# A retention and feed-forward kernel: a new load and cast prologue, a block-diagonal state product, score matmuls placed beside value matmuls, and the queries of the first four chunks loaded on the ScalarE queue

## The chip, the cores and the metric

The kernel runs on one core of one Trainium2 chip. The metric is device time in microseconds (us). The kernel before takes 239.28 us, the median of three runs (238.09 to 240.16). Each run is marked fast or slow; unless a text says otherwise, the runs compared here are fast ones.

"The profile" is a recording of one run of a kernel on the chip. PE is the matmul engine (TensorE), PEld its weight loads, DVE is VectorE, ACT is ScalarE, POOL is GpSimd, SP is SyncE. A name with a q behind it, such as ACTq, is the sequencer of that engine, which also issues DMA transfers. "Span" is the time from the first to the last instruction of the core; a timed run is longer than its span here (237.42 against 235.7 for the profiled run of before).

## The reference

```python
# q, k, v: 4 batches, 8 heads, 768 positions, 64 channels; fp32
gamma = 1.0 - 2.0 ** (-5.0 - np.arange(H))
for t in range(S):
    state = gamma * state + outer(k[:, :, t], v[:, :, t])     # 64 x 64 per head
    y[:, :, t] = (1 / sqrt(D)) * (q[:, :, t] @ state)
x = y.transpose(0, 2, 1, 3).reshape(B * S, H * D)              # 3072 x 512
h = np.maximum(x @ w_in, 0)                                    # w_in: 512 x 2048
return (h * h) @ w_out                                         # w_out: 2048 x 512
```

## The kernel before

The 3072 rows are cut into 24 chunks of 128, six for each batch. For a chunk, k is scaled by a decay factor and cast (`a_cast`), k and q are transposed on PE (`a_turn`), the masked scores inside the chunk are made (`a_score`), and `a_out` adds the state product (what earlier chunks of the batch contribute), the value product, and the update of the state. The feed-forward (`f1`, `f2`) takes four chunks at a time, in groups of four matmuls of 512 columns; the attention pieces of the next four chunks are woven between these groups. The parts that the argument touches:

```python
    blocks = [[0, 1], [2, 3]]          # then four chunks each
    # ... cut
    def load_chunk(m):
        b, i = divmod(m, NCH)
        got = []
        for name, src, dt in (("kn", k, FP32), ("qs", q, BF16), ("vs", v, BF16)):
            t = ldpool.tile([P, H, D], dt, tag=name, name=f"{name}{m}")
            eng = nc.sync if dt == FP32 else nc.gpsimd       # GpSimd's loads cast on the way
            eng.dma_start(t[:], src[b, :, i * C : (i + 1) * C, :].rearrange("h s d -> s h d"))
            # ... cut
    # ... cut: load_chunk(0) to (3) and constants between them, then the four slices of w_in,
    #     all on GpSimd's queue but k
    # in a_out(m): the state product, eight matmuls of 64x64
        if i > 0:
            s_bf = state["s"]
            for p in range(NP):
                for hh in range(2):
                    r = slice(64 * hh, 64 * hh + 64)
                    nc.tensor.matmul(yt[r, p, :], lhsT=s_bf[r, p, :], rhs=kqT[r, 1, p, :],
                                     start=(p == 0), stop=False, skip_group_check=True)
    # ... cut
    def stages(ms):                    # the order of the pieces that are woven in
        seq = []
        for n in range(len(ms) + 2):
            if 0 <= n - 1 < len(ms):
                seq.append(lambda m=ms[n - 1]: a_score(m))
            if n < len(ms):
                seq.append(lambda m=ms[n]: a_cast(m))
                seq.append(lambda m=ms[n]: a_turn(m))
            if 0 <= n - 2 < len(ms):
                seq.append(lambda m=ms[n - 2]: a_out(m))
        return seq
```

## Time and profile before

| profiled run of before | value |
|---|---|
| time, span | 237.42 us, 235.7 us (this run is 1.9 us under the median) |
| PE's first work | 9.55 us |
| first feed-forward matmul | 22.68 us |
| four blocks of four chunks | 35.09, 34.87, 34.75, 35.10 us |
| last block, nothing woven in | 27.79 us |
| end of PE, then the last store | 232.06 us, 3.6 us |

Two rows of the page of before. A digit is the busy share of one fortieth of the span, in tenths; PEclk is the granted clock of TensorE.

```profile
PE   0166997799999999999999999999999999999993
...
PEclk9999999999999999999999999999999999999999
```

PE is full from about slice 9 to the end (a slice is 5.9 us). The losses lie in the first fifth.

The chain of waits of before, two pieces of its first 25 us (start, length, what); the pieces ahead of them are mostly GpSimd issuing the loads of q and v. The chain runs back from the last instruction through whatever released each step.

```profile
11.97 10.67 DMA w_in_bf_93<-in_moe_w_in_dram
22.68 1.03 PE hp_0_348 L282 x4
```

The feed-forward can't start before the first slice of w_in is there, and that slice takes 10.67 us from its issue. Its first packet moves at 16.3, 4.3 us after the issue: until then GpSimd's queue carries the q and v loads that stand ahead of w_in. After that it shares the DMA engines with the loads of the chunks. The DMA view of before for 17 to 22 us shows how (queue, packets, MB, share of the engines); q0 is GpSimd's queue, with w_in, and q1 is Sync's, with k:

```profile
q0 software_dynamic: 913, 0.76, 93.3%
q1 hardware_dynamic: 839, 0.21, 32.0%
```

Both queues move about the same number of packets, but those of q1 have 256 bytes (0.21 MB over 839), so Sync's queue gets about 42 GB/s (0.21 MB in 5 us).

The table of windows of before: the stretch, its length, the busy time (and instructions) of PE, PEld, DVE, ACT and POOL, then granted clock, DMA share and GB/s.

```profile
22.68:45.37 22.69, 19.83 (x217) 15.63 (x218) 13.26 (x38) 14.81 (x36) 11.06 (x13) 1.00 1.59 190
...
99.55:134.42 34.87, 34.82 (x281) 16.84 (x280) 16.24 (x28) 17.05 (x28) 7.01 (x8) 1.00 0.70 91
...
204.27:232.06 27.79, 27.79 (x129) 12.44 (x127) 6.81 (x16) 11.95 (x20) 0.00 (x0) 1.00 0.10 38
```

A block of four chunks (34.87 us) is the 27.79 us of its feed-forward and 7.1 us of attention for the next four chunks, and PE is busy in all of it, by ends that are modelled. So in these blocks only less PE work helps, or less of the loss between its pieces, which this column doesn't show (next).

One chunk's `a_out` in such a block, from the timeline of PE in before (start, length, line, output and inputs, shapes). A matmul's recorded end is modelled, so read the distances between starts.

```profile
130.06 1.03 PE L301 MATMUL op_1700<-w_out_bf_97,h_3_1355 128*128 128x512 bf16 x4
131.01 0.41 PE L225 MATMUL yt_1705<-kqT_1596,s_1691 64*64 64x128 bf16 x8
131.35 0.41 PE L236 MATMUL yt_1705<-pt_1655,vs_1345 128*64 128x128 bf16 x8
131.60 0.29 PE L252 MATMUL c_1530<-vs_1345,ks_1573 128*64 128x64 bf16 x8
131.82 1.04 PE L301 MATMUL op_1700<-w_out_bf_98,h_3_1355 128*128 128x512 bf16 x4
```

The feed-forward group takes 0.95 us to the next start where two such groups in a row take 0.86: about 0.1 us is lost on entering this piece, which has another shape. The state product takes 0.34, the value product 0.25, the state update 0.22.

Entering the transposes, whose shape is the feed-forward's 128x128, costs nothing in itself (0.86, for example from 120.44 to 121.30). But in each full block those of the second and third chunk start 1.05 us after the group ahead of them, because the cast of k is not done (timeline of before; the group ahead starts at 105.61):

```profile
106.66 0.23 PEld L184 LDWEIGHTS <-ks_1413 128*128 128x128 bf16 x4 [0.51 <-DVE ks_1413 L171]
106.66 0.40 PE L184 MATMUL tp_1429<-ident,ks_1413 128*128 128x128 bf16 x4
```

That is 0.19 us, six times in the three blocks: 1.1 us.

### The profile page before, as it was taken

The page shows a single profiled execution, that of the slowest core. Times are in us where ns is not written, and L with a number is a line of the kernel's source. Part 1 is how long each engine was busy: PE and PEld are TensorE (multiplying, and loading weights), DVE is VectorE, ACT ScalarE, POOL GpSimd, SP SyncE. Part 2 cuts the span into 40 slices and gives each one's busy share as a digit, 9 for nine tenths or more (in the row PEclk, how much of TensorE's full clock was granted, in tenths as well). Part 3 has the DMA queues.
Part 4 walks back from the last instruction along what each step waited for, and adds up shares of the span by engine and source line. Part 5 has one row for each costly group of instructions (what it writes and reads, how often), then busy time and mean ns, then how long its engine had stood idle before and what let it go on. Part 6 is the DMA issues. An engine that isn't in the chain of part 4 may idle for free.

```text
span 235.7 us, 4145 instructions
## 1 busy us (share of the span) xinstructions
PE 214.2 (91%) x1728; PEld 110.9 (47%) x1728; DVE 101.4 (43%) x188; ACT 109.6 (46%) x190; POOL 51.5 (22%) x82
## 2 busy tenths in 40 slices
PE   0166997799999999999999999999999999999993
PEld 0145785454544444444445544444544554444441
DVE  0446665642356533356634266534266524144100
ACT  2292586432277721277722277621377622277221
POOL 8983155642410102410203410100000000000000
PEclk9999999999999999999999999999999999999999
DMA  8999999998994087993078992041170011100112
GB/s 130 215 191 197 198 181 190 185 161 127 138 183 79 3 89 87 111 185 65 4 88 91 112 194 54 2 64 47 46 178 4 0 47 46 63 29 0 42 47 89
DMA packets 82579, 23.34 MB, mean 99 GB/s; under 512 B 75392, under 2 KB 79488, under 8 KB 82560
## 3 DMA queue, kind: packets, MB, share of 16 engines
q0 software_dynamic: 54144, 10.49, 52.7%
q1 hardware_dynamic: 28416, 12.59, 20.3%
q8 instruction: 13, 0.21, 0.4%
q14 instruction: 6, 0.05, 0.1%
HBM read 27.26 MB, written 6.29 MB: 142 GB/s over the span
## 4 chain that ended last, share of the span: by engine, by line
PE 85%; DMA 5%; POOL 4%; DVE 2%; ACT 1%; issue 1%; ACTq 0%; POOLq 0%
DMA w_in_bf_93<-in_moe_w_in_dram 5%; PE op_2057 L301 2%; PE op_1641 L301 2%; PE op_1232 L301 2%; PE op_865 L301 2%; PE op_795 L301 2%; PE op_2470 L301 2%; PE op_2411 L301 2%; PE op_762 L301 2%; PE op_2378 L301 2%; PE op_1549 L301 2%; PE op_1140 L301 2%; PE op_2529 L301 2%; PE op_2008 L301 2%; PE op_1975 L301 2%; PE op_1700 L301 2%
## 5 line engine op out<-in xcount | busy, mean ns | idle before, releaser
L282 PEld LDWEIGHTS <-w_in_bf_93 128*128 128x128 bf16 x112 | 10.6, 101 | 9.6 <-DMA w_in_bf_93<-in_moe_w_in_dram 1.0
L282 PEld LDWEIGHTS <-w_in_bf_95 128*128 128x128 bf16 x112 | 10.5, 98 | 9.3
L282 PEld LDWEIGHTS <-w_in_bf_94 128*128 128x128 bf16 x112 | 10.6, 98 | 8.9
L282 PEld LDWEIGHTS <-w_in_bf_96 128*128 128x128 bf16 x112 | 10.3, 98 | 8.2
L290 DVE TENSOR_TENSOR h_6_2567<-h_6_2567 128x512 bf16<-128x512 bf16 x16 | 6.8, 426 | 10.1 <-ACT h_6_2567 L289 10.1
L290 DVE TENSOR_TENSOR h_5_2177<-h_5_2177 128x512 bf16<-128x512 bf16 x16 | 6.8, 424 | 9.4 <-ACT h_5_2177 L289 9.4
L290 DVE TENSOR_TENSOR h_4_1774<-h_4_1774 128x512 bf16<-128x512 bf16 x16 | 6.8, 424 | 9.4 <-ACT h_4_1774 L289 9.4
L290 DVE TENSOR_TENSOR h_2_939<-h_2_939 128x512 bf16<-128x512 bf16 x16 | 6.8, 423 | 9.4 <-ACT h_2_939 L289 9.4
L290 DVE TENSOR_TENSOR h_3_1355<-h_3_1355 128x512 bf16<-128x512 bf16 x16 | 6.8, 424 | 8.9 <-ACT h_3_1355 L289 8.9
L301 PEld LDWEIGHTS <-h_6_2567 128*128 128x128 bf16 x64 | 6.3, 98 | 7.5
L184 PE MATMUL tp_172<-ident,ks_170 128*128 128x128 bf16 x4 | 0.6, 307 | 9.6 <-DVE ks_170 L171 9.6
L301 PEld LDWEIGHTS <-h_4_1774 128*128 128x128 bf16 x64 | 5.8, 98 | 6.5
L301 PEld LDWEIGHTS <-h_2_939 128*128 128x128 bf16 x64 | 5.8, 98 | 6.5
L301 PEld LDWEIGHTS <-h_5_2177 128*128 128x128 bf16 x64 | 5.8, 98 | 6.5
L301 PEld LDWEIGHTS <-h_3_1355 128*128 128x128 bf16 x64 | 5.8, 98 | 6.5
L290 DVE TENSOR_TENSOR h_1_528<-h_1_528 128x256 bf16<-128x256 bf16 x16 | 4.6, 291 | 4.8 <-ACT h_1_528 L289 3.7
L290 DVE TENSOR_TENSOR h_0_347<-h_0_347 128x256 bf16<-128x256 bf16 x16 | 4.5, 291 | 4.8 <-ACT h_0_347 L289 3.5
L184 PEld LDWEIGHTS <-ks_170 128*128 128x128 bf16 x4 | 0.3, 130 | 9.5 <-DVE ks_170 L171 9.5
L301 PEld LDWEIGHTS <-h_1_528 128*128 128x128 bf16 x32 | 2.8, 98 | 3.1
L158 ACT ACTIVATE yf<-t_f,lnp 128x128 f32<-128x128 f32 (+1 forms) x8 | 4.2, 603 | 0.0
L301 PEld LDWEIGHTS <-h_0_347 128*128 128x128 bf16 x32 | 2.9, 98 | 2.8
L83 POOL DMA_DIRECT2D vs_2173<-in_v_dram x1 | 0.9, 876 | 13.9 <-PE c_1530 L252 13.9
(803 smaller groups left out, 516.5 us busy)
## 6 DMA issues: line engine op xcount, KB each, us to landing
w_in_bf_93<-in_moe_w_in_dram POOLq DMA_DIRECT2D x1, 512.0 KB, 10.7
w_in_bf_94<-in_moe_w_in_dram POOLq DMA_DIRECT2D x1, 512.0 KB, 13.2
w_in_bf_95<-in_moe_w_in_dram POOLq DMA_DIRECT2D x1, 512.0 KB, 15.2
w_in_bf_96<-in_moe_w_in_dram POOLq DMA_DIRECT2D x1, 512.0 KB, 17.1
w_out_bf_97<-in_moe_w_out_dram POOLq DMA_DIRECT2D x1, 512.0 KB, 17.6
w_out_bf_98<-in_moe_w_out_dram POOLq DMA_DIRECT2D x1, 512.0 KB, 13.7
w_out_bf_99<-in_moe_w_out_dram POOLq DMA_DIRECT2D x1, 512.0 KB, 11.8
w_out_bf_100<-in_moe_w_out_dram POOLq DMA_DIRECT2D x1, 512.0 KB, 11.6
```

What stands on the lines that cost most here:

```text
L83: eng.dma_start(t[:], src[b, :, i * C : (i + 1) * C, :].rearrange("h s d -> s h d"))
L158: nc.scalar.activation(yf[:, p, lo:hi], t_f[:, lo:hi], AF.Exp, scale=lnp[:, p : p + 1])
L184: nc.tensor.transpose(tp[:, j, p, :], src[:, 2 * p : 2 * p + 2, :], ident[:])
L282: nc.tensor.matmul(hp[:, :n], lhsT=w_in_bf[s][:, cb, r * P : (r + 1) * P], rhs=xts[b][:, cb, :n], start=(cb == 0), stop=(cb == NCB - 1),)
L290: nc.vector.tensor_mul(h2[:, fb, :n], h2[:, fb, :n], h2[:, fb, :n])
L301: nc.tensor.matmul(op[:], lhsT=h2s[b][:, fb, j * P : (j + 1) * P], rhs=w_out_bf[part][:, r, :], start=(fb == 0), stop=(fb == NFB - 1),)
```

## The change

The intent is to shorten the front and to take PE work out of the blocks.

- q, k and v of the first eight chunks come as fp32 on hardware queues, and engines cast them (q of chunks 0 to 3 on ScalarE, v on GpSimd). GpSimd's queue is then free for w_in. The queries of chunks 0 to 3 go over ScalarE's queue: q0 and q1 at the start, q2 and q3 after the second transposes, behind the copy of `kqT1` in ScalarE's stream. k and v of chunks 0 to 3 go over Sync's.
- Filler matmuls on a zero tile are meant to keep PE's clock up (`Z`). The order of the first 8 chunks is written out by hand (`run`), with blocks of 2, 2, 1, 3 and then 4 chunks.
- The state is kept block-diagonal for each pair of heads: four matmuls of 128x128 instead of eight of 64x64, at the price of a second small copy on ScalarE.
- From chunk 12 on, the score of chunk m+1 stands directly behind the value product of chunk m, and the cast runs one round ahead of its transposes.

Smaller edits come with it: some constants are filled on VectorE instead of GpSimd, and buffer counts differ.

```diff
-    blocks = [[0, 1], [2, 3]]
+    for n in (2, 2, 1, 3, 4, 4, 4, 4):
 ...
-    load_chunk(0)
+    load(nc.sync, "k", 0)
+    load(nc.scalar, "q", 0)
+    load(nc.sync, "v", 0)
+    load(nc.scalar, "q", 1)
+    for m in range(1, 4):
+        load(nc.sync, "k", m)
+        load(nc.sync, "v", m)
 ...  (in a_cast)
+        if m < FIRST:                                    # FIRST = 8
+            if m < 4:
+                nc.scalar.activation(qs[m][:], qn.pop(m)[:], AF.Copy)
+            else:
+                nc.gpsimd.tensor_copy(qs[m][:], qn.pop(m)[:])
+            nc.gpsimd.tensor_copy(vs[m][:], vn.pop(m)[:])
 ...  (in a_out)
-                for hh in range(2):
-                    r = slice(64 * hh, 64 * hh + 64)
-                    nc.tensor.matmul(yt[r, p, :], lhsT=s_bf[r, p, :], rhs=kqT[r, 1, p, :], ...)
+                nc.tensor.matmul(yt[:, p, :], lhsT=s_bd[i % 2][:, p, :], rhs=kqT[:, 1, p, :], ...)
 ...
+        if after is not None:
+            a_score(after)
 ...  (the prologue: K cast, T turn, S score, P out, Y decay fill, Z filler, F f1, G f2)
+    run("Y0 Z12 K0 T0 Y1 Z2 K1 S0 Z2 T1")
+    load(nc.scalar, "q", 2)
+    load(nc.scalar, "q", 3)
+    run(" P0 K2 S1 Y2 Z2 T2")
+    load_w_in(0)
+    load_w_in(1)
+    run("P1 K3 S2 Y3 Z2 T3 P2 S3 Y4 Z4")
+    for s in (2, 3):
+        load_w_in(s)
 ...  (w_out, then k, q, v of chunks 4 to 7, held until slice 2 of w_out has landed)
+    run("F0.0 P3 Y5 F0.1 F0.2 F0.3 F1.0 F1.1 F1.2 F1.3")
 ...
+    run("K4 G0.3 G1.3 G2.3 K5 T4 G3.0 S4 G3.1 T5 G3.2 P4 S5 G3.3 K6")
 ...
-            if n < len(ms):
-                seq.append(lambda m=ms[n]: a_cast(m))
-                seq.append(lambda m=ms[n]: a_turn(m))
+            if m + 1 < NCHUNK:
+                seq.append(lambda m=m: a_turn(m + 1))
+            if m + 2 < NCHUNK:
+                seq.append(lambda m=m: cast(m + 2))
+            seq.append(lambda m=m: a_out(m, m + 1 if m + 1 < NCHUNK else None))
```

## The prediction

> **What bounds it now.** From about 47 us to 232 us TensorE is the limit: the table of windows shows PE busy 10.0 of each 10 us, and a steady block of four chunks takes 34.9 us (64.5 to 204.2 us, four blocks). Of that, 32 feed-forward groups of four 512-column matmuls at 0.864 us are 27.7 us; attention takes 7.2, 1.8 us a chunk. The loss is in front. In the timeline TensorE does nothing until 9.55 us and starts the feed-forward at 22.68 us, when the first w_in slice lands (10.7 us after issue, in the chain of waits). From there to the end of TensorE (232.1) are 209.4 us, of which I count 204 as work; the rest is a cold start (the first 256-column matmuls take 213 ns each, from 25.8 us on 110) and waits for chunk casts near 38 to 43 us (PE busy 3.4 of 5 us, 8.6 of 10).
>
> **What changes in the steady part.** (a) The state product: 8 matmuls of 64x64 (0.35 us) become 4 of 128x128; four such transposes take 0.22 us: -0.13 us a chunk. (b) Score directly behind value saves one entry gap of about 0.1 us from chunk 12 on. (c) The cast is now one round ahead of its transposes; before, about half of them waited 0.1 to 0.2 us. Together about -0.25 us a chunk over 20 chunks: -5 us. ScalarE gains one small copy a chunk (0.37 us now); at 48% busy that costs nothing.
>
> **What changes in front.** q, k, v of chunks 0 to 3 come as fp32 on hardware queues, which move 230 to 240 GB/s when alone (packet records, 2 to 4 us): 256 KB in 1.1 us, so v2 lands near 11.3 us. Casts go to ScalarE (q, est. 0.6 us, from the 128x512 output copy) and GpSimd (v, est. 0.8 us, unmeasured). w_in then starts about where it does now, 12 us, but with nothing ahead of it in its queue: landing near 18 instead of 22.7. The new limit is the attention chain through ScalarE: per chunk 1.0 us eviction, 0.6 cast, 1.3 decay fill; and the issue of q2 and q3 stands behind the second eviction, near 11.5 us. That is late: once w_in packets flow, the trace shows hardware-queue packets alternating 1:1 with w_in's (154 against 154 per us, 39 GB/s, 17 to 26 us); the Trainium skill's "DMA: Bandwidth & Descriptors", Queues, rings and completion order, describes this round robin. q3 may thus take 6.5 us instead of 1.1, landing near 20.5; then cast, fill, eviction, score, filler: feed-forward starts near 25 (22.4 if q3 is early, 28 if q2 suffers too). By then only the last value product of the four chunks is left.
>
> **Sum.** Start 25 + work left about 199 + stalls 3 (cold clock, decay fill holding relus, the one-chunk block) + tail 3.6 = 230.6 us of span, against 235.7; with the same 2 to 3 us outside the span: 233. The fillers should warm the clock (skill, "TensorE: Matmul & The Clock Gate", Part 1: a few us of activity), if idle gaps do not undo it.
>
> **Checks.** Steady block near 33.8 us; state product near 0.22 us; q3 landing 6 us or more after issue; first feed-forward matmul 22 to 28 us; no wait for k4.
>
> **What would make it wrong.** q2 and q3 landing before w_in flows (then 230); both crawling, with a cold TensorE (237); slow GpSimd casts delaying w_in.
>
> Chances: faster by over 2% 0.66, within 2% 0.29, slower 0.05. Predicted 233, range 228 to 237.5.

## The result, and the profile after

The changed kernel takes 230.12 us, the median of four runs (229.41 to 230.88), against 239.03 us for the kernel before in the same rounds (four runs). The ratio is 0.9626, with a 95% interval of 0.9571 to 0.9681. Ratios here are the mean time of one kernel's fast runs over that of the other's fast runs of the same rounds, so not quite the quotient of the medians. The profiled run (229.41 us) is the fastest of the four.

The page of after:

```profile
span 227.6 us, 4271 instructions
...
PE   7649799999879999999999999999999999999993
...
PEclk9997999999999999999999999999999999999999
```

PE works from the first slice on (fillers), and its clock falls in the fourth slice.

The chain of waits of after, long pieces in the first 25 us:

```profile
10.22 3.35 DMA qn_246<-in_q_dram
...
23.42 1.28 ACT yf_169 L175 x4
```

w_in has left the chain. In its place stand the load of q2 (`qn_246`), issued at 10.22, and ScalarE's work.

The timeline of after at these places (sequencer, engines; in brackets the idle time before and what ended it):

```profile
10.22 0.37 ACTq L91 DMA_DIRECT2D qn_246<-in_q_dram  x1
10.63 0.60 ACTq L91 DMA_DIRECT2D qn_248<-in_q_dram  x1
11.35 0.89 POOL L96 DMA_DIRECT2D w_in_bf_96<-in_moe_w_in_dram  x1
13.59 0.63 ACT L207 ACTIVATE qs_274<-qn_246 128x512 bf16<-128x512 f32 x1 [1.47 <-DMA qn_246<-in_q_dram]
14.27 0.40 PE L220 MATMUL tp_297<-ident,qs_274 128*128 128x128 bf16 x4 [1.82 <-ACT qs_274 L207]
21.25 0.60 PE L319 MATMUL hp_0_443<-xt_250,w_in_bf_96 128*128 128x256 bf16 x4
25.16 0.60 PE L319 MATMUL hp_0_499<-xt_250,w_in_bf_96 128*128 128x256 bf16 x4 [1.20 <-ACT h_0_442 L326]
```

ScalarE waits 1.47 us for q2, and PE 1.82 us for the cast of q2. The feed-forward starts at 21.25. At 25.16 PE waits 1.20 us, because the decay fill at 23.42 (in the chain above) holds ScalarE, which has to take the feed-forward's results out of PSUM.

How the queues shared the DMA engines in after: first 10.5 to 14 us, where q10 is ScalarE's queue with q2 and q3, q1 Sync's, and q0 w_in's:

```profile
q10 hardware_dynamic: 2064, 0.52, 65.7%
q1 hardware_dynamic: 1323, 0.33, 41.9%
q0 software_dynamic: 22, 0.02, 4.6%
```

q2 and q3 (0.52 MB together) moved almost wholly before the packets of w_in flowed. w_in is issued at 11.35, only 0.6 us earlier than in before: its issue stands in GpSimd's stream behind the cast of v2, which waits 1.78 us for v2. It starts to move at about 13.6, 2.2 us after the issue and not 4.3 as in before, and lands at 19.8.

The table of windows of after, the stretches that answer to those of before, with the same columns:

```profile
21.25:37.38 16.13, 14.93 (x149) 13.16 (x148) 9.76 (x32) 14.50 (x41) 0.00 (x0) 1.00 1.10 184
...
96.42:130.12 33.70, 33.70 (x272) 17.51 (x270) 15.96 (x28) 18.28 (x33) 6.99 (x8) 1.00 0.71 94
```

From the first feed-forward matmul to the first group of f2 it is now 16.13 us and was 22.69. The two stretches don't hold the same work: in before it has two `a_out` and a score of the first four chunks and the transposes and scores of chunks 4 and 5 in it, with two waits of 0.97 us for casts; in after it has one `a_out` and no wait for casts. PE is idle 2.86 us in the one and 1.20 in the other. A full block takes 33.70 us (the next one 33.57) instead of 34.87. The last full block takes 32.57: each block now makes transposes and a score for the next one as well, and the last has no next. So some of this work (transposes of chunks 12 and 13, score of chunk 12) now lies ahead of the first full block. It is worth 1.3 us, by two kernels below that differ there in nothing else: 28.39 us for the feed-forward of chunks 5 to 7 in a_state64, 27.06 in a_oldweave.

One `a_out` in a block of after:

```profile
115.75 1.03 PE L338 MATMUL op_1763<-w_out_bf_103,h_2_1544 128*128 128x512 bf16 x4
116.61 0.39 PE L256 MATMUL yt_1791<-kqT_1635,s_bd_170 128*128 128x128 bf16 x4
116.93 0.41 PE L267 MATMUL yt_1791<-pt_1722,vs_1418 128*64 128x128 bf16 x8
117.17 0.29 PE L283 MATMUL c_1598<-vs_1418,ks_1565 128*64 128x64 bf16 x8
117.40 0.40 PE L230 MATMUL st_1815<-kqT_1745 64*128 64x128 bf16 x8
117.73 1.04 PE L338 MATMUL op_1826<-w_out_bf_100,h_2_1544 128*128 128x512 bf16 x4
```

Entering the state product now costs nothing: the group before it takes 0.86 to the next start, not 0.95. The product takes 0.32 to the next start, so the lost 0.1 us has moved behind it, where the tile shape now changes. Group and state product took 1.29 us together and take 1.18. The score follows the state update at once. No transposes wait for a cast in the full blocks: all start 0.86 us after the group ahead of them.

Where the 8.0 us between the two profiled runs came from: the first feed-forward matmul is 1.43 us earlier (22.68 to 21.25), and from it to the end of PE it is 6.58 us less (209.38 to 202.80). The second figure mixes two things. From the start of the feed-forward of chunks 8 to 11 (99.55 before, 96.42 after) to the end of PE it was 132.51 and is 127.63; without the 1.3 us of work that had moved ahead of that point, about 3.5 us were gained there. The other 4.5 us were gained ahead of it, by the new prologue and by the state products of the first chunks.

### The profile page after: what moved, and what is told of

Its sections match the earlier page's. It is cut to its first block, busy times and chain, and to the rows that moved or that the text cites. A ratio compares the mean times of both kernels' runs of the same rounds, so it can differ in the third digit from the quotient of the medians.

```text
span 227.6 us, 4271 instructions
## 1 busy us (share of the span) xinstructions
PE 213.9 (94%) x1736; PEld 118.9 (52%) x1736; DVE 103.5 (45%) x221; ACT 123.3 (54%) x246; POOL 43.5 (19%) x62
## 3 DMA queue, kind: packets, MB, share of 16 engines
q10 hardware_dynamic: 4160, 1.05, 2.0%
## 4 chain that ended last, share of the span: by engine, by line
PE 87%; ACT 7%; DVE 2%; DMA 1%; issue 1%; ACTq 0%
PE fill L354 3%; PE op_2633 L338 2%; PE op_2223 L338 2%; PE op_1480 L338 2%; PE op_1072 L338 2%; PE op_2512 L338 2%; PE op_2317 L338 2%; PE op_1920 L338 2%; PE op_1826 L338 2%; PE op_1427 L338 2%; PE op_2860 L338 2%; PE op_705 L338 2%; PE op_700 L338 2%; PE op_2800 L338 2%; PE op_1857 L338 2%; PE op_1763 L338 2%
## 5 line engine op out<-in xcount | busy, mean ns | idle before, releaser
L319 PEld LDWEIGHTS <-w_in_bf_96 128*128 128x128 bf16 x128 | 11.6, 98 | 9.8 <-issue 1.4
L319 PEld LDWEIGHTS <-w_in_bf_98 128*128 128x128 bf16 x128 | 11.8, 98 | 8.6
L319 PEld LDWEIGHTS <-w_in_bf_99 128*128 128x128 bf16 x128 | 11.6, 98 | 8.2
L319 PEld LDWEIGHTS <-w_in_bf_97 128*128 128x128 bf16 x128 | 11.4, 98 | 8.0
L327 DVE TENSOR_TENSOR h_5_2687<-h_5_2687 128x512 bf16<-128x512 bf16 x16 | 6.8, 425 | 11.8 <-ACT h_5_2687 L326 11.8
L327 DVE TENSOR_TENSOR h_2_1544<-h_2_1544 128x512 bf16<-128x512 bf16 x16 | 6.8, 424 | 10.7 <-ACT h_2_1544 L326 10.6
L327 DVE TENSOR_TENSOR h_4_2348<-h_4_2348 128x512 bf16<-128x512 bf16 x16 | 6.8, 424 | 9.6 <-ACT h_4_2348 L326 9.6
L327 DVE TENSOR_TENSOR h_3_1951<-h_3_1951 128x512 bf16<-128x512 bf16 x16 | 6.8, 423 | 9.5 <-ACT h_3_1951 L326 9.5
L327 DVE TENSOR_TENSOR h_1_876<-h_1_876 128x128 bf16<-128x128 bf16 (+1 forms) x32 | 8.5, 289 | 5.5 <-ACT h_1_876 L326 5.4
L354 PE MATMUL fill<-zero 128*128 128x512 bf16 x24 | 9.2, 527 | 1.2 <-DVE zero L149 1.2
L338 PEld LDWEIGHTS <-h_5_2687 128*128 128x128 bf16 x64 | 6.3, 98 | 7.5
L338 PEld LDWEIGHTS <-h_3_1951 128*128 128x128 bf16 x64 | 6.1, 98 | 7.0
L338 PEld LDWEIGHTS <-h_2_1544 128*128 128x128 bf16 x64 | 6.0, 98 | 7.1
L338 PEld LDWEIGHTS <-h_4_2348 128*128 128x128 bf16 x64 | 6.0, 98 | 6.9
L338 PEld LDWEIGHTS <-h_1_876 128*128 128x128 bf16 x64 | 6.0, 98 | 6.8
L338 PEld LDWEIGHTS <-h_0_442 128*128 128x128 bf16 x64 | 6.0, 98 | 6.6
L347 ACT ACTIVATE osb_744<-op_695 128x512 f32<-128x512 f32 x1 | 0.6, 597 | 8.2 <-PE op_695 L338 8.2
L354 PEld LDWEIGHTS <-zero 128*128 128x128 bf16 x24 | 2.5, 122 | 4.7 <-issue 2.9
L256 PEld LDWEIGHTS <-s_bd_171 128*128 128x128 bf16 x48 | 3.6, 98 | 2.3
L209 POOL CAST qs_736<-qn_420 128x512 bf16<-128x512 f32 x1 | 0.6, 613 | 21.8 <-DMA qn_420<-in_q_dram 21.8
L238 DVE TENSOR_TENSOR pt_792<-st_783,cmask 128x1024 bf16<-128x1024 f32 x1 | 1.2, 1225 | 7.5 <-PE st_783 L230 7.5
## 6 DMA issues: line engine op xcount, KB each, us to landing
w_in_bf_99<-in_moe_w_in_dram POOLq DMA_DIRECT2D x1, 512.0 KB, 13.6
w_out_bf_101<-in_moe_w_out_dram POOLq DMA_DIRECT2D x1, 512.0 KB, 17.1
```

Source lines behind the costliest of these rows:

```text
L209: nc.gpsimd.tensor_copy(qs[m][:], qn.pop(m)[:])
L238: nc.vector.tensor_tensor(out=pt[:], in0=st[:], in1=cmask[:, None, None, :].to_broadcast([P, 2, NP, P]), op=ALU.mult,)
L256: nc.tensor.matmul(yt[:, p, :], lhsT=s_bd[i % 2][:, p, :], rhs=kqT[:, 1, p, :], start=(p == 0), stop=False, skip_group_check=True,)
L319: nc.tensor.matmul(hp[:, :n], lhsT=w_in_bf[s][:, cb, r * P : (r + 1) * P], rhs=xts[g][:, cb, cols], start=(cb == 0), stop=(cb == NCB - 1),)
L327: nc.vector.tensor_mul(h2[:, fb, cols], h2[:, fb, cols], h2[:, fb, cols])
L338: nc.tensor.matmul(op[:], lhsT=h2s[g][:, fb, j * P : (j + 1) * P], rhs=w_out_bf[part][:, r, :], start=(fb == 0), stop=(fb == NFB - 1),)
```

## The experiments

Twelve runs followed, one of them of the changed kernel again; all gave correct results. They ran in four groups, each on one chip with its own runs of the kernel before (medians 239.95, 239.14, 238.85 and 239.35 us), so read the ratios across groups and the times inside one. "Blocks" are the three full blocks of chunks 8 to 19, each from its first feed-forward matmul to that of the next. "Start" is the first feed-forward matmul, read from the one profiled run. Where a block column is blank, the blocks are those of after to 0.02 us.

| kernel | group | median us | ratio to before, 95% | start | blocks |
|---|---|---|---|---|---|
| after again | A | 230.31 | 0.9603 (0.9573 to 0.9634) | 22.68 | 33.70, 33.58, 32.57 |
| state product of eight | A | 232.59 | 0.9700 (0.9671 to 0.9728) | 22.44 | 34.06, 33.92, 33.05 |
| score apart | A | 230.92 | 0.9638 (0.9608 to 0.9667) | 21.31 | 34.13, 34.00, 32.89 |
| cast beside its transposes | A | 230.13 | 0.9599 (0.9569 to 0.9629) | 22.26 | 33.69, 33.58, 33.02 |
| before with the new blocks | B | 236.73 | 0.9886 (0.9857 to 0.9915) | 24.11 | 33.7, 33.57, 32.57 |
| all loads on Sync's queue | B | 228.00 | 0.9526 (0.9497 to 0.9555) | 19.87 | |
| w_in issued early | B | 235.86 | 0.9837 (0.9800 to 0.9874) | 29.71 (slow) | |
| no fillers | B | 229.93 | 0.9605 (0.9580 to 0.9631) | 21.00 | |
| decay fills late | C | 229.22 | 0.9584 (0.9547 to 0.9620) | 21.91 | |
| q2, q3 issued early | C | 228.32 | 0.9546 (0.9508 to 0.9584) | 20.12 | |
| combined | C | 225.79 | 0.9450 (0.9405 to 0.9495) | 19.95 | |
| old blocks, new prologue | D | 234.55 | 0.9802 (0.9762 to 0.9842) | 21.98 | 34.87, 34.75, 35.09 |

My theory had four parts. The front gains because w_in has GpSimd's queue to itself and casts no longer hold the first blocks. The blocks gain from three small cuts in PE's work. The late issue of q2 and q3 on ScalarE's queue costs something. And that cost would come from sharing the DMA engines with w_in. The rivals were that the fillers' warm clock is what brings the gain, and that the late issue or the second queue costs nothing (or gains).

### The changed kernel again (a_again)

No edit; it is the measure for its group.

> The changed kernel once more, unedited, as the yardstick of this group. Both theories: ratio to the kernel before 0.96, time near 230 us; four-chunk blocks (first matmul of one block's feed-forward to that of the next) 33.6 to 33.7 us while the next block's attention is woven in, first feed-forward matmul at 21.2 us.

Measured: 230.31 us, ratio 0.9603. Start came at 22.68 in this profile, 1.4 us later than in the first one, with the same program: PE's clock was halved for 6.8 us here (15.6 to 22.4) and for 3.4 us there. All six runs had a mean clock of 0.985, as three of the four earlier ones did; the run profiled as "after" (0.993) is the lucky kind. So in the usual run of this kernel the start is probably near 22.7, as it was in before's profile, and a difference of about 1 us between the starts of single profiles means nothing here. From the start to the end of PE, though, both profiles take 202.80 us, and so do a_qsync and a_qearly below, which change only what lies ahead of the start. What a kernel takes from its start on can thus be compared between single profiles.

### The state product back to eight matmuls (a_state64)

```diff
-                nc.tensor.matmul(yt[:, p, :], lhsT=s_bd[i % 2][:, p, :], rhs=kqT[:, 1, p, :], ...)
+                for hh in range(2):
+                    r = slice(64 * hh, 64 * hh + 64)
+                    nc.tensor.matmul(yt[r, p, :], lhsT=s_bd[i % 2][r, p, 64 * hh : 64 * hh + 64],
+                                     rhs=kqT[r, 1, p, :], ...)
```

> Only the state product is put back to eight 64x64 matmuls. Theory (the steady part gives about half of the gain, and this is its largest piece): the state group takes 0.35 us instead of 0.22 plus a switch of 0.1, so +0.05 to +0.15 us a chunk, blocks 33.9 to 34.1 us, time +1 to +2.5 us. Rival (the whole gain is in the first 100 us, the steady edits are noise): blocks stay at 33.6 us, time within 0.3 us of the changed kernel.

Measured: 232.59 us, 2.3 us more than the changed kernel on the same chip; the start differs by 0.24 us only. The full blocks are 0.34 to 0.36 us longer, the last 0.48. Twenty chunks have a state product (the first of each batch has none), so it is 0.11 us each: what the timelines of before and after show (1.29 against 1.18). From the start to the end of PE it is 204.81 us against 202.80, 2.0 us more. This is the largest single gain in the blocks.

### The score as a piece of its own (a_apart)

```diff
-            seq.append(lambda m=m: a_out(m, m + 1 if m + 1 < NCHUNK else None))
+            seq.append(lambda m=m: a_out(m))
+            if m + 1 < NCHUNK:
+                seq.append(lambda m=m: a_score(m + 1))
```

> Score and value products are separate pieces of the weave again in the last four blocks. Theory: one more entry gap of 0.1 us for each of about 11 chunks, so +0.4 us a block, +1 to +1.5 us in all. Rival (position does not matter, the switch from value to score costs as much as from feed-forward to score): blocks 33.6 us, no change.

Measured: 230.92 us, 0.6 us more. The blocks are 0.43, 0.42 and 0.32 us longer, about 0.1 us a chunk. The timeline of PE in this kernel shows the cost: 1.83 us to the score from the start of two groups that take 1.73 when another group follows.

```profile
116.80 1.90 PE L338 MATMUL op<-w_out_bf,h 128*128 128x512 bf16 x8
118.63 0.40 PE L230 MATMUL st<-kqT 64*128 64x128 bf16 x8
```

The three blocks sum to 1.17 us more, against 0.6 timed. Three of its six runs had the luckier clock (0.989 to 0.992), which none of the six of a_again had. The other three (0.984 or 0.985, as a_again) took 231.11 to 231.60 us, 0.8 to 1.3 more than a_again's median, which agrees with the trace. From the start to the end of PE it is 203.97 against 202.80, 1.17 us more.

### The cast beside its transposes (a_castlate)

```diff
-        while loaded[0] + 1 < NCHUNK and loaded[0] < m + 2:
+        while loaded[0] + 1 < NCHUNK and loaded[0] < m + 3:
 ...
-        a_cast(m)
+        if m > 13:
+            a_cast(m)
 ...
+                seq.append(lambda m=m: cast(m + 1))
                 seq.append(lambda m=m: a_turn(m + 1))
-            if m + 2 < NCHUNK:
-                seq.append(lambda m=m: cast(m + 2))
```

> The k cast of a chunk is again directly ahead of its transposes in the last four blocks. Theory: about half of the transposes wait 0.1 to 0.2 us for the cast, so +0.2 to +0.6 us a block, +0.5 to +1.5 us in all, visible as TensorE idle released by the cast. Rival: VectorE is free enough, no change.

Measured: 230.13 us, and blocks of 33.69 and 33.58: no difference. (The third takes 33.02 and not 32.57, but the block ahead of the three 0.44 less; from the start to the end of PE it is 202.81.) This did not undo what I meant to undo. With the score joined to `a_out` there are fewer pieces to weave in, so a feed-forward group still lies between a cast and its transposes, and PE doesn't wait. It says nothing about casts in the old order.

### Before, with the new blocks (b_steady)

The block-diagonal state and the new piece order in the kernel before; its prologue is left as it was.

```diff
 ...  (the block-diagonal state as in the change; chunk 9 loaded early)
-    weave(q1[NFB // 2 :] + all_f2(0) + all_f2(1), stages(blocks[2]))
+    weave(q1[NFB // 2 :] + all_f2(0) + all_f2(1),
+          stages(blocks[2]) + [lambda: a_cast(8), lambda: a_turn(8), lambda: a_cast(9), lambda: a_score(8)])
 ...
-        weave(all_f1(b) + all_f2(b), stages(blocks[b + 1]) if b + 1 < len(blocks) else [])
+        weave(all_f1(b) + all_f2(b), side(blocks[b + 1]) if b + 1 < len(blocks) else [])
```

> The kernel before, old prologue and old blocks, with only the steady edits: block-diagonal state, score behind value, cast one round ahead. Theory (half of the gain is steady): four-chunk blocks 33.6 to 33.8 us instead of 34.9, time 4 to 5 us under the kernel before, ratio 0.980 to 0.985. Rival (gain is all in front): ratio 0.997 to 1.003.

Measured: 236.73 us, 2.4 us under before. Its blocks are as long as those of after (33.7, 33.57, 32.57), so the block gain itself arrived. But its front is worse than that of before: start 24.11 against 22.68, first group of f2 at 50.79 against 45.37. From start to f2 it is 26.68 us against 22.69, since the four extra pieces were woven into a stretch that already waits for casts. The later start is w_in landing at 24.1 instead of 22.6, from an issue at the same time; why is not shown. The run mixes a gain and a new loss and can't size the blocks' share. a_oldweave, below, was made for that.

### All loads of chunks 0 to 3 on Sync's queue (a_qsync)

```diff
-    load(nc.sync, "k", 0)
-    load(nc.scalar, "q", 0)
-    load(nc.sync, "v", 0)
-    load(nc.scalar, "q", 1)
-    for m in range(1, 4):
-        load(nc.sync, "k", m)
-        load(nc.sync, "v", m)
+    for m in range(4):
+        for name in "kqv":
+            load(nc.sync, name, m)
 ...
-    load(nc.scalar, "q", 2)
-    load(nc.scalar, "q", 3)
```

> All first loads on the Sync queue in the order k, q, v; nothing on the ScalarE queue. Theory of the queue (ScalarE's late issue of q2 and q3 is harmless because they land before the weights flow): first transposes a little later, v2 lands about 2 us later because q1 and q2 stand ahead of it, the first w_in slice is issued at 13 to 14 us instead of 11.4 and lands at 21 to 22 us; first feed-forward matmul 22 to 23 us; time +0.5 to +1.5 us. Rival (my prediction's step: q2 and q3 on ScalarE are late and hold the chain): first feed-forward earlier than 21 us, time -1 us or better.

Measured: 228.00 us, ratio 0.9526 (0.9497 to 0.9555), about 2 us better than the changed kernel, whose interval in group A (0.9573 to 0.9634) lies wholly above. I had expected it to be slower, so this part of my theory fell: sending the queries over ScalarE's queue, with q2 and q3 issued late, costs about 2 us (1.8 to 2.4 by the ratios to before). The chain of waits of this kernel at the place where after waits for q2:

```profile
12.21 0.03 issue
12.23 0.63 ACT qs L203
```

ScalarE casts q2 at 12.23 with no wait (13.59 in after). w_in is issued later than in after (12.65, against 11.35), and the start still comes at 19.87: w_in was not the limit in after.

### w_in issued early (a_winearly)

The first two slices of w_in are issued at about 9.0 us, before q2 and q3 are on their way.

```diff
     load(nc.scalar, "q", 3)
-    run(" P0 K2 S1 Y2 Z2 T2")
     load_w_in(0)
     load_w_in(1)
+    run(" P0 K2 S1 Y2 Z2 T2")
```

> The first two w_in slices are issued on GpSimd ahead of the v2 cast, near 9 us instead of 11.4, so that their packets flow while q2, q3, k3 and v3 are still loading. Theory (packets of two queues alternate one for one, the hardware queue falls to about 40 GB/s beside w_in; only the timing saved q2 and q3): q2 lands after 16 us and q3 after 20 us (13.6 and 14.4 now), the third and fourth transposes wait for them, first feed-forward matmul 24 us or later although w_in lands by 18 us; time +2 to +5 us. Rival (the hardware queues keep their 250 GB/s beside w_in): q3 lands before 16 us, w_in near 17.5, feed-forward at 20 to 21, time the same or up to 1 us better.

Measured: 235.86 us over all six runs. Two of them are slow (238.74, 239.36), the profiled one too; the four fast ones are 234.87 to 236.46, with a ratio of 0.9837. Against the changed kernel (0.9603) that is about 5.5 us worse. The DMA view of the profiled run for 14 to 19 us, w_in on q0 and q2, q3 on q10:

```profile
q0 software_dynamic: 790, 0.79, 92.3%
q10 hardware_dynamic: 770, 0.20, 29.4%
```

and ScalarE's timeline:

```profile
18.01 0.63 ACT L207 ACTIVATE qs<-qn 128x512 bf16<-128x512 f32 x1 [7.00 <-DMA qn<-in_q_dram]
...
24.59 0.63 ACT L207 ACTIVATE qs<-qn 128x512 bf16<-128x512 f32 x1 [3.06 <-DMA qn<-in_q_dram]
```

Packets are shared one for one (790 against 770), and a packet of w_in has 1000 bytes where one of q has 256, so q2 and q3 crawl at 40 GB/s (0.20 MB in 5 us) and ScalarE waits 7.0 and 3.1 us for them. The mechanism is read from this profile, the size from the fast runs. This is the sharing that the prediction feared. It is real, and the changed kernel just escapes it: in after q2 is in at 13.6 and q3 at 14.4, as the packets of w_in begin. The Trainium skill, "DMA: Bandwidth & Descriptors", Queues, rings and completion order, has each DMA engine go round the queues packet by packet; equal packet counts agree with that.

### No fillers (a_nofill)

```diff
     def fill(n):
-
+        return
```

> The filler matmuls of the prologue are gone. Theory (they keep the TensorE clock up and cost nothing otherwise): [...]first transposes at 5.4 instead of 6.3 us, but attention steps take twice as long; net +0.5 to +1.5 us. Rival (the fillers are in the way: twelve cold ones hold the first transposes 0.9 us and the rest sit in a chain that ScalarE limits): time -0.5 us or better.

Measured: 229.93 us, ratio 0.9605 (0.9580 to 0.9631), the same as with the fillers. Without them PE runs its early attention work slowly (cold until 22.8 us, by the durations of its matmuls), but starts that work earlier: start is 21.00. The rival that the fillers bring the gain is out, and so is any sizeable cost of them. A warning about reading: the clock column stands at 1.00 during this cold stretch, as it does over the cold first 25 us of before, and dips only where the clock falls again later. So the mean clock compares only kernels that start in the same way.

### The decay fills late (a_decaylate)

```diff
-    run("P1 K3 S2 Y3 Z2 T3 P2 S3 Y4 Z4")
+    run("P1 K3 S2 Y3 Z2 T3 P2 S3 Z4")
-    run("F0.0 P3 Y5 F0.1 ...")
+    run("F0.0 P3 F0.1 ...")
-    run("K4 G0.3 ...")
+    run("Y4 Y5 K4 G0.3 ...")
```

> The last two decay fills (1.28 us each on ScalarE) move from the start of the feed-forward to the stretch near 37 us, where ScalarE waits 8 us for the first output. Theory: the 1.2 us in which TensorE waits for relus behind the fill (at 24 to 25 us) goes, and the first relu comes up to 1.2 us sooner; time -1.0 to -1.5 us against 230.3. Rival (the weights then set the pace, w_in slices landing every 2.5 to 3 us): no change.

Measured: 229.22 us, ratio 0.9584. The wait of 1.2 us that after has at 25.16 is gone, and from the start to the first group of f2 it is 14.86 us instead of 16.13. The ratio is 0.002 to 0.004 under those of after (0.9603, 0.9626), 0.5 to 1.0 us, inside the intervals' overlap; the trace's 1.27 us is the better measure, since this stretch is 16.13 in after, a_again, a_qsync and a_qearly alike.

### q2 and q3 on ScalarE's queue, but issued early (a_qearly)

```diff
-    run("Y0 Z12 K0 T0 Y1 Z2 K1 S0 Z2 T1")
+    run("Y0")
     load(nc.scalar, "q", 2)
     load(nc.scalar, "q", 3)
+    run("Z12 K0 T0 Y1 Z2 K1 S0 Z2 T1")
```

This tells a second queue apart from a late issue.

> q2 and q3 stay on the ScalarE queue, but are issued near 4.7 us, behind the first decay fill, instead of 10.2 us behind the second eviction. Theory (the loss of 2.2 us against one Sync queue is the late issue: ScalarE waits 1.5 us for q2, TensorE idles 2 us and its clock drops to half): as fast as one Sync queue, 227.5 to 228.5 us, q2 cast without a wait, clock whole from 7 us on. Rival (the second queue itself, or ScalarE's time for issuing, costs it): 229.5 to 230.5 us.

Measured: 228.32 us, ratio 0.9546 (0.9508 to 0.9584): within the error of one Sync queue (0.9526). Against the changed kernel (0.9603, 0.9626) it is 1.4 to 1.9 us better; the interval just touches that of a_again (0.9573 to 0.9634). q2 is cast at 12.47 with no wait, and start comes at 20.12 (21.25 and 22.68 in the changed kernel). So the second queue itself costs next to nothing and brings nothing; the late issue was the fault. The Trainium skill says the same, "DMA: Bandwidth & Descriptors", Issuing engines are not separate DMA queues: spreading loads over issuing engines saves only the issue time. Here even that is doubtful, for the issue is work for ScalarE: the chain of waits shows it issuing until 6.40, and the cast of q0 right after it at 6.45.

### The parts that helped, combined (best)

a_qsync, with `Y4 Y5` moved as in a_decaylate, the last fillers cut from four to two, and the cast of chunk 8 one piece earlier (after waits 1.27 us for it at 68 us).

```diff
-    run("P1 K3 S2 Y3 Z2 T3 P2 S3 Y4 Z4")
+    run("P1 K3 S2 Y3 Z2 T3 P2 S3 Z2")
 ...
-    weave(all_f1(2) + all_f2(2), [... "T7", "S7 L9")])
+    weave(all_f1(2) + all_f2(2), [... "T7", "S7 L9 K8")])
```

> One Sync queue, decay fills 4 and 5 late, half of the last filler removed, and the cast of chunk 8 one piece earlier (its transposes wait 1.3 us for it at 67 us). If the parts add to the 228.0 us of one Sync queue: -1.2 for the decay fills, -0.4 to -0.6 for a feed-forward start at 19.3 us, -1.2 for the cast: 225 to 225.5 us. If w_in then sets the pace of the first feed-forward groups: 226.5 us.

Measured: 225.79 us, ratio 0.9450 (0.9405 to 0.9495): 5.5% under before and about 4 us under the changed kernel. The timeline of PE shows what limits its front now:

```profile
19.95 0.61 PE L315 MATMUL hp<-xt,w_in_bf 128*128 128x256 bf16 x4 [1.17 <-DMA w_in_bf<-in_moe_w_in_dram]
```

PE waits 1.17 us for w_in: with attention early enough, the weights are the limit again.

### The old blocks behind the new prologue (a_oldweave)

From chunk 12 on the old order of pieces (`stages`), and the state product of eight matmuls throughout; all else as after.

```diff
-                nc.tensor.matmul(yt[:, p, :], lhsT=s_bd[i % 2][:, p, :], rhs=kqT[:, 1, p, :], ...)
+                (eight of 64x64, as in a_state64)
 ...
-    ... "T11 L13,P10 S11 L14,P11 K12,T12 L15,S12,K13"
+    ... "T11 L13,P10 S11 L14,P11,L15"
 ...
-            side(blocks[b + 1]) if b + 1 < len(blocks) else [],
+            stages(blocks[b + 1]) if b + 1 < len(blocks) else [],
```

> The new prologue with the old steady part from chunk 12 on: the piece order of the kernel before (score, cast, transposes, value two chunks behind), and eight 64x64 state matmuls everywhere. Theory (about 4 us of the gain is steady): four-chunk blocks back at 34.7 to 35.1 us, time 233.5 to 235 us, that is 3.3 to 4.5 over the changed kernel's 230.2. Rival (the steady part is only what the single undos showed, 2.3 for the state and 0.6 for the score): 232.8 to 233.2 us.

Measured: 234.55 us, ratio 0.9802. Its blocks are 34.87, 34.75 and 35.09, within a hundredth those of before from chunk 8 on (34.87, 34.75, 35.10), so this undoes the change of the blocks. (The state products of the first chunks are put back too.) The new prologue alone is worth 2.0% (4.7 us), with an interval of 1.6 to 2.4%; between the two profiled runs it is 2.9 us, that of before being 1.9 us under its median. No run takes the prologue apart further, but for its queries, fillers and decay fills. The rest, 0.9802 to 0.9603 or 0.9626, is 0.0176 to 0.0199, or 4.2 to 4.8 us, and belongs to the steady part. Undone one at a time, the state product is worth 2.3 us and the joined score 0.6 to 1.2. That leaves 0.7 to 1.9 us for the rest of the piece order, and the errors of these ratios are as large. The profiles are sharper. From the start to the end of PE a_oldweave takes 207.16 us, 4.36 more than after. Of that the state product is 2.01 and the joined score 1.17, which leaves 1.18. The traces show what that is: the same six waits of transposes for the cast as in before (1.05 us from the group ahead instead of 0.86, 1.1 us in all), and none in after. No run undoes the cast's place alone (a_castlate failed to), so this part rests on the traces.

### What made the late issue cost 2 us

The wait for q2 comes first. ScalarE casts q2 at 13.59 in after (idle 1.47 us) and at 14.18 in a_again (idle 2.61, and PE 2.96), against 12.23 in a_qsync. PE's clock comes second. The table of windows, for three stretches of 3.4 us: first after, in the stretch ahead of the drop and the one of the drop,

```profile
13.30:16.70 3.40, 1.30 (x32) 1.09 (x32) 1.29 (x2) 3.08 (x7) 3.40 (x6) 1.00 1.12 187
```

```profile
16.70:20.10 3.40, 3.36 (x40) 2.31 (x36) 1.44 (x2) 3.21 (x8) 1.27 (x2) 0.50 1.24 205
```

then a_qsync, in the like stretch:

```profile
13.90:17.30 3.40, 2.11 (x42) 1.39 (x36) 2.52 (x3) 3.33 (x9) 2.63 (x5) 1.00 0.99 158
```

In after PE was busy 1.30 of 3.40 us, and the clock in the stretch that follows is 0.50. In a_qsync it was busy 2.11, and no drop follows. The drops of one profile lie on a raster of 3.413 us: in after at 16.68 and, past the end of PE's work, at 228.31, 62 steps apart. On this raster the stretches ahead of a drop had 0.33 to 1.57 us busy (a_state64 0.33, a_again 0.73, a_apart 1.09, a_oldweave 1.21; 1.57 in b_steady, whose clock drops at 47.31). Stretches at full clock with no drop behind them had 1.83 or more (a_qearly 1.83 at 5.05, before 1.88 at 39.32, after 1.94 at 9.86, best 1.95, a_qsync 2.12). The half clock lasts 3.4 or 6.8 us, which differs between runs of one program, and 17.1 in a_winearly. It ended after one stretch where PE was busy for 3.02 us or more of it (a_oldweave 3.02, a_apart 3.05, after 3.37), and not where it was busy for 2.99 or less (a_decaylate 2.99, a_again 2.47).

How much each is worth can be read off the starts. In after q2 is cast 1.36 us later than in a_qsync and the feed-forward starts 1.38 us later (21.25 against 19.87): 3.4 us of half clock added nothing, for ScalarE set the pace. In a_again the cast is 1.95 us later and the start 2.81: 6.8 us of half clock added about 0.9. These are single profiles, so this split is rough. Sharing with w_in has no part in it in after, where q2 is in as w_in's first packet moves. In a_again it may have a small one: from 13 to 14 us it moved 699 packets of q and 28 of w_in, but these 28 took 41% of the engines' time, and q2 landed at 14.2. Nor is the issue alone what counts: in the kernels that issue q2 late it is issued anywhere from 9.1 to 10.3 us and lands at 13.6 to 14.3, without the earlier being the sooner. What holds it between issue and landing is not shown.

## Why the prediction was right or wrong

It gave 233 us, with a range of 228 to 237.5. The kernel takes 230.12, inside the range and 2.9 us below the point. The prediction was a sum, so its terms can be set beside the profiled run of after:

| term of the sum | predicted us | measured us |
|---|---|---|
| start of the feed-forward | 25 | 21.25 (22.68 in a_again) |
| from there to the end of PE ("work left about 199 + stalls 3") | 202 | 202.80 |
| tail | 3.6 | 3.55 |
| outside the span | 2 to 3 (1.72 in before) | 1.81 |

**The start was mis-sized; the rest of the sum held.** (Work and stalls can be compared only together.) The step that failed is "q3 may thus take 6.5 us instead of 1.1, landing near 20.5". It took 3.8 us and landed at 14.4. I had put the issue "near 11.5 us"; it came at 10.22 and 10.63. And I had w_in flowing "about where it does now, 12 us"; its packets began at 13.6, 2.2 us after the issue (1.6 to 3.0 us in all profiles of this prologue), and the sum had no such delay. Between 10.5 and 14 us w_in moved 22 packets, and q2 and q3 2064. So the crawl did not happen. The prediction named this way of being wrong ("q2 and q3 landing before w_in flows (then 230)"), and that is what came: 230.12.

**The mechanism behind the failed step was right.** Packets do alternate one for one, and q2 and q3 do crawl when w_in is ahead of them: a_winearly shows 790 packets against 770, 40 GB/s, and 5.5 us lost. It was put where it did not apply, by a margin of next to nothing.

**The late issue did cost, by another way.** It was called "late" in the prediction, and rightly. a_qsync and a_qearly agree on about 2 us, but through ScalarE's wait for q2 and, in most runs, PE's clock, and not, or only at its very end in a_again, through w_in. When I saw that q3 was early, I concluded that the order was harmless and expected a_qsync to be slower. That was wrong too.

**The blocks.** Predicted: "Steady block near 33.8 us" and -5 us over 20 chunks. Measured: 33.70 and 33.57, and 4.2 to 4.8 us by a_oldweave's times, 4.36 by its profile. Of its parts: (a) 0.13 us a chunk, measured 0.11; the product itself is the 0.22 us of its shape, but the loss on a change of shape, 0.1 us, now stands behind it. (b) 0.1 us a chunk, measured 0.1. (c) the cast a round ahead: "about half of them waited 0.1 to 0.2 us" is six of twelve in the traces, 0.19 us each, 1.1 us in all; no run shows it alone.

**The front.** "Landing near 18 instead of 22.7" for w_in: it landed at 19.8 in after and at 17.6 in a_again, so the estimate was fair and the lucky profile has the later landing. The change of limit, from w_in to the chain through ScalarE, was right: the chain of waits of after holds q2 and ScalarE's work, and no w_in. "Decay fill holding relus" was right (1.20 us at 25.16; a_decaylate takes it away). "No wait for k4" was right on PE: no wait for it stands in the chain. "Slow GpSimd casts delaying w_in" did not come: a cast of v takes 0.61 us, and it is v2's landing that holds w_in's issue till 11.35. The Trainium skill, "GPSIMD Engine Reference", 4.1, calls one-input work on GpSimd roughly line-rate, compared with VectorE; here a 128x512 cast took 0.61 us there and 0.63 on ScalarE, and no run makes it on VectorE, so this doesn't contradict the page but is no test of it. "The fillers should warm the clock" was right about the clock early on and wrong about its worth (a_nofill: none), and "if idle gaps do not undo it" was the part that came true.

## What to carry to other kernels

When a load is moved to another queue, ask first where its issue stands in that engine's stream: behind an engine's own work it starts late, and here that cost 2 us where the second queue itself cost nothing. Small-packet loads must be in before a large-packet load starts on another queue, since the engines share by packet and not by byte. And before a new shape or order is put into a full engine, read the starts of neighbouring groups: 0.1 us at each change of shape, times 20 chunks, is 2 us, as much as the late issue cost.

## What the Trainium skill lacked or had wrong

- "TensorE: Matmul & The Clock Gate", Part 1, lets the clock fall after at least one idle window of about 3.4 us. Here it fell after windows in which PE was busy for 0.33 to 1.57 of 3.4 us (after: 1.30, and the clock then 0.50; b_steady: 1.57), with longest idle gaps of 1.16 us (b_steady), 1.82 us (after) and 3.12 us (a_state64), none of them a whole window. Windows with 1.83 us or more kept it. The page also tells of a kernel whose frequent short idles brought drops, but gives no such share. Busy time here is partly modelled, so the limit between 1.57 and 1.83 is rough. What the page says of a free-running window and of luck between runs agrees: one program was at half clock for 3.4 us in one run and for 6.8 in another.
- "DMA: Bandwidth & Descriptors", Queues, rings and completion order, has the round robin but not what it does to a queue of small packets: 256-byte packets beside w_in's of 1000 bytes got 40 GB/s (a_winearly, 770 packets against 790), where the hardware queues alone moved 275 GB/s (after, 6 to 10 us).
- "DMA: Bandwidth & Descriptors", Issuing engines are not separate DMA queues, was borne out (0.9546 against 0.9526), but lacks that an issue waits behind the issuing engine's own work: in after q2 was issued at 10.22 behind ScalarE's copies, and 1.4 to 2.4 us were lost against either early issue (ratios 0.9546 and 0.9526 against 0.9603 and 0.9626).
- "TensorEngine Tiling (Array Packing)", Key Properties, says that a change of tiling mode drains TensorE, without a size. Here it is about 0.1 us: a group of four 512-column matmuls takes 0.95 to the next start ahead of a 64x64 piece (before, 130.06), and 0.86 ahead of a 128x128 one (after, 115.75; before, 120.44).
